# Building the decay of the first seven chunks from operands already on the chip

## The chip, the cores and the metric

One core of a Trainium2 chip runs the whole program. Its engines are TensorE (PE in the profile), VectorE (DVE), ScalarE (ACT), GpSimd (POOL) and SyncE (SP), which only issues transfers here. The metric is the device time of one execution in microseconds (us). Before the change it is 658.33 us, the median of 3 runs (658.04 to 658.83).

## The reference

Three layers follow one another: a chunked state-space scan with 4 batches, 8 heads, 768 positions, head size 32 and state size 16, then a feed-forward layer (256 to 2048 to 256, leaky), then a gated one (256 to 1536 to 256). Only the scan is touched by the change.

```python
log_a = np.log(np.clip(a, 1e-06, 1.0))
for c in range(nc):
    cum = np.cumsum(la, axis=-1)
    L = np.exp(cum[:, :, :, None] - cum[:, :, None, :]) * causal
    CB = np.einsum('bhin,bhjn->bhij', Cc, Bc)
    y_intra = np.einsum('bhij,bhjd->bhid', CB * L, xc)
    y_inter = np.einsum('bhin,bhnd->bhid', Cc, state) * np.exp(cum)[:, :, :, None]
    state = decay_full * state + np.sum(Bx, axis=2)
```

The reference's chunk is 32 positions long; the kernel works with chunks of 96, which gives the same sums.

## The kernel before

The scan has 32 chunks of T = 96 positions (8 per batch). For each chunk four steps are issued. `ev_scores` makes the scores C times B in the PSUM tile `cb`. `ev_decay` makes the exponents cum_i - cum_j plus a causal mask in the PSUM tile `d`, for 8 heads by 96 positions (two products of 384 columns), and ScalarE takes their exponential into `lt`. `ev_weigh` multiplies both into `mt` on VectorE and scales B into `bd`. `ev_out` multiplies `bd` and `mt` with x (tile `yd`); ScalarE copies the new state into the next chunk's x tile `xs` in four small copies and the output into `x1`. `cb` and `d` have one buffer each, so the scores of a chunk wait for the `mt` of the chunk before, and its decay for the `lt` of the chunk before.

The decay product has one left operand `dl` (114 x 112: a unit matrix, two rows of ones, and 16 rows of cum_j, two parts per head) and one right operand `dr` (114 x 768: the mask, two rows of cum_i, and 16 rows of head signs). There are NC = 4 pairs of them. The fixed part of each is copied from `misc` by ScalarE and VectorE (lines 562 to 574); the cum rows come by transfers: for chunks 0 to 2 straight from the tile `parts` (lines 260 to 266), for all later ones through a buffer in device memory, `cum_d` (written at line 291, read at 267 and 270).

The program order is written out by hand: each engine executes its own instructions strictly in the order in which the loop issues them, and SyncE's transfers likewise. The loop runs over chunks i and issues `ev_weigh(i)`, loads of chunk i + 3, `ev_decay(i + 1)`, a share of the weight preparation (`feed`: raw 64-bit words to two 32-bit parts, on VectorE and ScalarE, with raw tiles loaded through GpSimd's queue), `ev_out(i - 1)` and `ev_scores(i + 1)`. After the first 7 chunks, the lead, 512 positions are complete, and from then on each turn also issues a step of the first feed-forward layer (`h` and `acc`). The halves of its first activations are the tiles `xh`; the first half is split by ScalarE and VectorE at chunk 3, the second at chunk 6.

The steps that the change and the prediction touch: the first loads (lines 549 to 560), the set-up of the logarithms, scans and operands (lines 561 to 628), `load_cum` (257), `ev_decay` (297) and the loop's first turns (634 on).

Of the kernel before, what the change touches and what calls it, by code (L numbers as in the profile page):

```python
# [8 lines left out]
F32 = mybir.dt.float32  # L9
# [31 lines left out]
NC = 4  # L41
# [6 lines left out]
def kernel(  # L48
# [159 lines left out]
    DIRECT = 3  # L208
# [13 lines left out]
    picks = x1[0:1, 0, NT - S - 2 * NR:NT - S].rearrange("p (r l) -> p r l", l=2)  # L222
    xs = [apool.tile([W, H * (D + N)], F32, name=f"xs{i}") for i in range(NX)]
# [33 lines left out]
    def load_cum(c):  # L257
        b, k = divmod(c, CPB)
        s = slice(k * T, (k + 1) * T)
        if c < DIRECT:  # L260

            rows = bf(parts[2 * b * H:2 * (b + 1) * H, s])
            for l, e in enumerate((nc.sync, nc.scalar if c < 2 else nc.sync)):
                e.dma_start(out=bf(dr[c % NC][T + l:T + l + 1]), in_=rows[l:2 * H:2])
            nc.sync.dma_start(out=bf(dl[c % NC][T + 2:KD, 0:T]), in_=rows)
            return
# [30 lines left out]
    def ev_decay(c):  # L297

        d = psum.tile([W, 2, 512], F32, tag="d", name="d")
        for e in range(2):  # L300
            nc.tensor.matmul(  # L301
                d[:, e, 0:4 * T], dl[c % NC], dr[c % NC][:, 4 * e:4 * e + 4, :],
                start=True, stop=True,
            )
# [203 lines left out]
    with tc.manual_schedule():  # L508
# [24 lines left out]
        for j in range(NG):  # L533
            nc.gpsimd.memset(ct[j], 0.0)
        warm = apool.tile([2 * NR, 2], F32, name="warm")

        def load_a(e, s):
            for l in range(2):
                e.dma_start(
                    out=a_t[l:2 * NR:2, s], in_=a.rearrange("b h s -> (b h) s")[:, s]  # L540
                )
# [11 lines left out]
        nc.sync.dma_start(out=misc, in_=k_misc[:, c0:])  # L553
        load_bc(0)
        load_x(0)
        take_up(1)
# [4 lines left out]
        seen = apool.tile([128, 2], F32, name="seen")  # L561

        def setup_dl(i):
            nc.scalar.copy(dl[i], left_c)

        def setup_mask(i, e):
            (e.copy if e is nc.scalar else e.tensor_copy)(
                dr[i][0:T], mask_c.unsqueeze(1).broadcast_to([T, H, T])
            )

        def setup_heads(i):
            nc.vector.tensor_copy(
                dr[i][T:KD], heads_c.unsqueeze(2).broadcast_to([KD - T, H, T])
            )
# [8 lines left out]

        clip_a(pieces[0])
        log_a(pieces[0])
        scan(pieces[0])
        setup_heads(0)
        halve_cum(pieces[0], nc.scalar)
        setup_dl(0)
        load_cum(0)  # L590
        clip_a(slice(T, S))
        log_a(slice(T, S))
        setup_mask(0, nc.vector)
        ev_scores(0)
        nc.scalar.activation(warm[:, 1:2], ones_t[:, 0:1], AF.Exp)
        scan(pieces[1])
        halve_cum(pieces[1], nc.vector)
        setup_dl(1)
        setup_mask(1, nc.scalar)
        setup_heads(1)  # L600
        load_bc(1)
        load_cum(1)
        load_x(1)

        nc.gpsimd.tensor_copy(seen[T:KD, 0:1], bf(dl[1][T:KD, 0:1]))
        ev_decay(0)
        take_up(2)
        setup_dl(2)
        setup_mask(2, nc.scalar)
        setup_heads(2)  # L610
        scan(pieces[2])
        load_cum(2)
        halve_cum(pieces[2], nc.vector)
        load_bc(2)
        load_x(2)
        store_cum()
# [7 lines left out]
        for j in range(3, NX):  # L624
            load_eye(j)
# [149 lines left out]
```

## Time and profile before

| | |
|---|---|
| median of 3 runs | 658.33 us |
| the profiled execution's own time | 659.65 us |
| its span, first to last instruction | 657.9 us |
| TensorE busy | 631.5 us (96%) |
| VectorE, ScalarE, GpSimd busy | 389.2, 333.5, 33.5 us |
| mean granted TensorE clock | 0.996 |
| bytes moved | 31.03 MB |

TensorE is busy 96% of the span. The page's slices are 16.4 us long; the first three of them hold most of its idle time. A timeline row gives the start, the length, the engine, the line, what is written from what, the shapes and how many instructions were merged; in brackets stands how long the engine was idle before and what released it.

### The profile page before, as it was taken

Reading aid. Unit: us, or ns where it says so; the run is one execution under the profiler, and the core shown is the slowest. Engines: PE = TensorE matmul, PEld = TensorE weight load, DVE = VectorE, ACT = ScalarE, POOL = GpSimd, SP = SyncE. Lnnn points to the kernel's source line nnn. Section 1 sums busy time; section 2 is a strip of 40 time slices with the busy share of each in tenths; the row PEclk is TensorE's granted clock in tenths of the full one; section 3 lists DMA queues with packets and bytes.
Section 4 is the critical chain, followed back from the end, with each engine's and each line's share of the span. In section 5 each row is a group of like instructions: output and inputs, shape, how many; then the busy total and the mean of one; then the engine's idle time right before and its main releaser. Section 6 shows DMA issues by size and latency. Waiting matters only on the chain.

```text
span 657.9 us, 9595 instructions
## 1 busy us (share of the span) xinstructions
PE 631.5 (96%) x3744; PEld 500.2 (76%) x3744; DVE 389.2 (59%) x636; ACT 333.5 (51%) x628; POOL 33.5 (5%) x54
## 2 busy tenths in 40 slices
PE   2789999999999999999999999999999999999997
PEld 1346666667888888888888888888888888888885
DVE  6489988775887888777586333433433433433432
ACT  5588877776656656665565332332332332332322
POOL 4201101000000000000000000000000000000000
PEclk9989999999999999999999999999999999999999
DMA  4764444410111211220000000100000100100000
GB/s 131 219 203 123 133 127 120 116 55 2 52 45 64 65 50 47 65 64 1 0 1 0 1 1 0 33 1 0 33 0 1 33 0 1 33 0 1 32 1 32
DMA packets 19799, 31.03 MB, mean 47 GB/s; under 512 B 7466, under 2 KB 15274, under 8 KB 19754
## 3 DMA queue, kind: packets, MB, share of 16 engines
q0 software_dynamic: 5152, 17.89, 8.9%
q1 hardware_dynamic: 14394, 12.36, 6.5%
q8 instruction: 29, 0.48, 0.3%
q10 hardware_dynamic: 208, 0.18, 0.1%
q14 instruction: 16, 0.13, 0.1%
HBM read 27.04 MB, written 3.34 MB: 46 GB/s over the span
## 4 chain that ended last, share of the span: by engine, by line
PE 89%; DVE 5%; ACT 3%; issue 1%; DMA 1%; ACTq 0%
PE acc L433 20%; PE h L394 19%; PE gate L460 15%; PE val L460 15%; PE po L488 10%; PE po L493 5%; PE cb L320 3%; PE d L301 1%; DVE mt L327 1%; PE yd L355 1%; DMA dr<-cum_d 1%; PE yd L349 1%; ACT xs L362 1%; DVE raw L168 0%; DVE x L278 0%
## 5 line engine op out<-in xcount | busy, mean ns | idle before, releaser
L394 PE MATMUL h<-xh,win 128*128 128x512 f32 x576 | 146.9, 391 | 1.0 <-ACT xh L385 1.0
L467 DVE TENSOR_TENSOR p<-val,s 128x512 f32<-128x512 f32 x72 | 49.8, 691 | 138.5 <-PE val L460 136.7
L394 PEld LDWEIGHTS h<-xh,win 128*128 128x128 f32 x576 | 107.7, 188 | 22.9 <-ACT xh L385 1.3
L433 PE MATMUL acc<-gh,wout 128*128 128x512 f32 x384 | 105.8, 397 | 0.0
L401 DVE SCALAR_TENSOR_TENSOR g<-h,salpha,t 128x512 f32<-128x512 f32 x96 | 71.9, 749 | 39.6 <-ACT t L399 39.1
L460 PE MATMUL gate<-xh,w2gate 128*128 128x512 f32 x360 | 92.8, 393 | 0.0
L410 ACT CAST gh<-p 128x512 fp32r<-128x512 f32 x72 | 44.6, 620 | 93.5 <-DVE p L467 93.5
L460 PE MATMUL val<-xh,w2val 128*128 128x512 f32 x360 | 91.3, 389 | 0.0
L465 ACT ACTIVATE s<-gate 128x512 f32<-128x512 f32 x72 | 43.0, 597 | 93.1 <-PE gate L460 93.1
L433 PEld LDWEIGHTS acc<-gh,wout 128*128 128x128 f32 x384 | 70.1, 188 | 26.3 <-ACT t L399 11.2
L399 ACT ACTIVATE t<-h,sign 128x512 f32<-128x512 f32 x96 | 66.0, 688 | 42.6 <-PE h L394 41.8
L410 ACT CAST gh<-g 128x512 fp32r<-128x512 f32 x96 | 59.6, 621 | 42.2 <-DVE g L401 42.2
L460 PEld LDWEIGHTS val<-xh,w2val 128*128 128x128 f32 x360 | 67.6, 188 | 14.3
L411 DVE TENSOR_TENSOR gl<-g,gh 128x512 fp32r<-128x512 f32 x96 | 66.0, 688 | 15.3 <-ACT gh L410 14.3
L411 DVE TENSOR_TENSOR gl<-p,gh 128x512 fp32r<-128x512 f32 x72 | 49.7, 691 | 41.2 <-ACT gh L410 41.1
L460 PEld LDWEIGHTS gate<-xh,w2gate 128*128 128x128 f32 x360 | 63.9, 189 | 10.6
L488 PE MATMUL po<-w2out,gh 128*128 128x512 f32 x240 | 64.1, 389 | 0.0
L433 PE MATMUL acc<-gl,wout 128*128 128x512 f32 x192 | 59.2, 390 | 0.0
L488 PEld LDWEIGHTS po<-w2out,gh 128*128 128x128 f32 x240 | 45.0, 188 | 9.4
L433 PEld LDWEIGHTS acc<-gl,wout 128*128 128x128 f32 x192 | 36.0, 188 | 7.9
L493 PEld LDWEIGHTS po<-w2out,gl 128*128 128x128 f32 x240 | 36.7, 189 | 4.7
L493 PE MATMUL po<-w2out,gl 128*128 128x256 f32 x240 | 38.1, 282 | 0.0
(84 smaller groups left out, 566.2 us busy)
## 6 DMA issues: line engine op xcount, KB each, us to landing
raw<-in_moe_w_out_dram POOLq DMA_DIRECT2D x14, 512.0 KB, 4.1
xs<-in_xb_dram SPq DMA_DIRECT2D x32, 144.0 KB
raw<-in_moe_w_in_dram POOLq DMA_DIRECT2D x8, 512.0 KB, 4.8
raw<-in_moe_w_gate_dram POOLq DMA_DIRECT2D x6, 512.0 KB, 4.4
raw<-in_moe_w_val_dram POOLq DMA_DIRECT2D x6, 512.0 KB, 4.1
out_dram<-osb SPq DMA_DIRECT2D x12, 256.0 KB
bt<-in_bc_dram SPq DMA_DIRECT2D x7, 192.0 KB
ct<-in_bc_dram SPq DMA_DIRECT2D x28, 48.0 KB
```

What stands on the lines that cost most here:

```text
L320: nc.tensor.matmul(cb[:, e, 0:4 * T], left, right, start=True, stop=True)
L394: nc.tensor.matmul(h, w[:, wl, kt, :], xh["m1", k][:, xl, kt, :], start=(i == 0 and kt == 0), stop=(i == 2 and kt == KT - 1),)
L399: nc.scalar.activation(t, h, AF.Identity, scale=sign[:, f:f + 1])
L401: nc.vector.scalar_tensor_tensor(g, h, salpha[:, f:f + 1], t, op0=ALU.mult, op1=ALU.max)
L410: nc.scalar.copy(gh, g)
L411: nc.vector.tensor_tensor(gl, g, bf(gh), op=ALU.subtract)
L433: nc.tensor.matmul(acc[k][:, m], w[:, wl, m * 128:(m + 1) * 128], g, start=(first and i == 0), stop=(last and i == 2),)
L460: nc.tensor.matmul(p, w[:, wl, kt, :], xh["m2", k][:, xl, kt, :], start=(i == 0 and kt == 0), stop=(i == 2 and kt == KT - 1),)
L465: nc.scalar.activation(s, gate, AF.Sigmoid)
L467: nc.vector.tensor_tensor(p, val, s, op=ALU.mult)
L488: nc.tensor.matmul(o[e][:, u].rearrange("p (l d) -> p l d", l=2), ph[:, ts], w, start=(f == 0), stop=False, skip_group_check=True,)
L493: nc.tensor.matmul(o[e][:, u, 0:DM], pl[:, ts], w[:, 0, :], start=False, stop=last, skip_group_check=True,)
```

## The change

For chunks 0 to 6 (`DIRECT = 7`) the decay is no longer built from `dl` and `dr`. A left operand `early_l` holds, for all seven chunks side by side, the unit matrix and the 16 rows of cum_j, which VectorE copies from `parts`; a right operand `early_r` holds the mask and the head signs. One product of 384 columns gives the mask and the cum_j part; the cum_i part is added by four products of 96 columns with `early_i` (16 x 112 per head) on the left and `parts` on the right. With two halves a chunk has two products of 384 and eight of 96 columns. The three operands lie in weight tiles (`win[-1]`, `wout[-1]`, `wout[-2]`) that are not yet in use. The direct transfers from `parts` into `dl` and `dr` are gone; chunks 7 and later still use `dl` and `dr`, of which there are now 3 pairs, set up by `setup_decay` in the loop at chunks 1 to 3. The scans of positions 288 to 767 move behind `ev_weigh(0)`. The logarithms come in two pieces at the start, the loads of a, misc, B, C and x are issued in another order, and GpSimd clears `ct[1]` after its first weight load.

```diff
+            if c >= DIRECT:
+                nc.tensor.matmul(
+                    d[:, e, 0:4 * T], dl[c % NC], dr[c % NC][:, hs, :], start=True, stop=True
+                )
+                continue
             nc.tensor.matmul(
-                d[:, e, 0:4 * T], dl[c % NC], dr[c % NC][:, 4 * e:4 * e + 4, :],
-                start=True, stop=True,
-            )
+                d[:, e, 0:4 * T], early_l[:, c], early_r[:, hs, :],
+                start=True, stop=False, skip_group_check=True,
+            )
+            for q in range(4):
+                nc.tensor.matmul(
+                    d[:, e, q * T:(q + 1) * T], early_i[:, 4 * e + q],
+                    parts[0:2 * H, c * T:(c + 1) * T],
+                    start=False, stop=True, skip_group_check=True,
+                )
...
-        load_a(nc.sync, pieces[0])
-        load_a(nc.scalar, slice(T, S))
-        nc.scalar.dma_start(out=pick, in_=picks)
+        for l, e in enumerate((nc.sync, nc.scalar)):
+            e.dma_start(out=a_t[l:2 * NR:2], in_=a.rearrange("b h s -> (b h) s"))
+        nc.sync.dma_start(out=pick, in_=picks)
+        nc.scalar.dma_start(out=misc, in_=k_misc[:, c0:])
+        nc.scalar.dma_start(out=neg, in_=k_misc[T + 2:KD, c0:c0 + H])
...
+        nc.gpsimd.memset(ct[1], 0.0)
+        take_up(2)
...
         clip_a(pieces[0])
         log_a(pieces[0])
+        clip_a(rest)
+        log_a(rest)
+        nc.scalar.activation(
+            early_i, neg.unsqueeze(2).broadcast_to([2 * H, H, W]), AF.Copy, scale=-1.0
+        )
+        nc.scalar.copy(
+            early_l[0:T], left_c[0:T].unsqueeze(1).broadcast_to([T, DIRECT, W])
+        )
...
+        def later_cum():
+            scan(pieces[2])
+            halve_cum(pieces[2], nc.scalar)
+            early_cum(pieces[2])
+            store_cum()
+            for j in range(3, NX):
+                load_eye(j)
+            setup_alpha()
+
+        def setup_decay(j):
+
+            nc.scalar.copy(dl[j], left_c)
+            nc.scalar.copy(dr[j][0:T], mask_c.unsqueeze(1).broadcast_to([T, H, T]))
+            nc.sync.dma_start(out=bf(dr[j][T + 2:KD]), in_=bf(early_r[T:W]))
...
             if i == 0:
+                later_cum()
+            if i == 1:
...
-            if i + 4 < NCH:
-                load_cum(i + 4)
+            if DIRECT <= i + 3 < NCH:
+                load_cum(i + 3)
...
+            if 0 < i <= NC:
+                setup_decay(i - 1)
```

TensorE, from the values of chunk 0 (`yd`) to the scores of chunk 3 (`cb`), before; `d` is the decay of chunk 3 there:

```order
L349 MATMUL yd<-xs_102,bd 16x32 x8
L355 MATMUL yd<-mt,xs_102 32x96 x8
L320 MATMUL cb<-bct 112x384 x2
L301 MATMUL d<-dr_115,dl_111 112x384 x2
L349 MATMUL yd<-xs_103,bd 16x32 x8
L355 MATMUL yd<-mt,xs_103 32x96 x8
L320 MATMUL cb<-bct 112x384 x2
```

The same place after; `wout_89` is the tile under `early_r`, `win_81` that under `early_l`, `wout_88` that under `early_i`:

```order
L362 MATMUL yd<-xs_103,bd 16x32 x8
L368 MATMUL yd<-mt,xs_103 32x96 x8
L333 MATMUL cb<-bct 112x384 x2
L308 MATMUL d<-wout_89,win_81 112x384
L313 MATMUL d<-parts,wout_88 112x96 x4
L308 MATMUL d<-wout_89,win_81 112x384
L313 MATMUL d<-parts,wout_88 112x96 x4
L362 MATMUL yd<-xs_104,bd 16x32 x8
L368 MATMUL yd<-mt,xs_104 32x96 x8
L333 MATMUL cb<-bct 112x384 x2
```

The decay between the scores of chunk 2 and the values of chunk 1 has grown from two products to ten, of which eight have 96 columns.

ScalarE, from the exponential of chunk 2 to the output copy of chunk 1, before (`mag` and `win` are weight preparation):

```order
L306 ACTIVATE lt<-d 112x768
L362 COPY xs_103<-yd 16x2x32 x4
L363 COPY x_73<-yd 128x2x96
L133 ACTIVATE mag<-raw 128x512
L306 ACTIVATE lt<-d 112x768
L148 CAST win_74<-mag 128x512
L362 COPY xs_104<-yd 16x2x32 x4
L363 COPY x_73<-yd 128x2x96
```

And after:

```order
L319 ACTIVATE lt<-d 112x768
L375 COPY xs_104<-yd 16x2x32 x4
L376 COPY x_73<-yd 128x2x96
L133 ACTIVATE mag<-raw 128x512
L631 CAST dl_109<-misc 114x112
L632 CAST dr_112<-misc 96x768
L319 ACTIVATE lt<-d 112x768
L148 CAST win_74<-mag 128x512
L375 COPY xs_105<-yd 16x2x32 x4
L376 COPY x_73<-yd 128x2x96
```

The two copies that fill a `dl` and a `dr` now stand between the weight scaling and the exponential of chunk 3; before, all of them stood ahead of the loop. The same pair stands once more in each of the next two turns.

SyncE, from the store of the cum rows on, before:

```order
L291 DMA cum_d<-parts 64x768
L267 DMA dl_111<-cum_d 16x96
L270 DMA dr_115<-cum_d 2x8x96
L237 DMA xs_105<-in_xb_dram 96x384
L246 DMA bct<-in_bc_dram 128x496
L267 DMA dl_108<-cum_d 16x96
L270 DMA dr_112<-cum_d 2x8x96
```

And after:

```order
L292 DMA cum_d<-parts 64x768
L245 DMA xs_106<-in_xb_dram 96x384
L254 DMA bct<-in_bc_dram 128x496
L245 DMA xs_107<-in_xb_dram 96x384
L257 DMA bt_115<-in_bc_dram 128x4x96
L263 DMA ct_117<-in_bc_dram 32x384 x4
L633 DMA dr_112<-wout_89 16x768
```

Behind the store, the cum rows of chunks 3 and 4 stood between the loads of x and C; now the loads of x, B and C follow at once.

## Rows read from the trace of the kernel before

**Rows 1.** Page, slices: busy tenths of TensorE in 40 slices of 16.4 us
```profile
PE   2789999999999999999999999999999999999997
```

**Rows 2.** Windows: length, busy us of PE, PEld, DVE, ACT, POOL, clock, DMA share, GB/s
```profile
20.00:30.00 10.00, 5.92 (x56) 2.42 (x59) 3.67 (x8) 4.10 (x13) 2.10 (x4) 1.00 0.89 257
...
30.00:40.00 10.00, 8.47 (x140) 4.17 (x136) 8.01 (x17) 8.21 (x23) 1.72 (x3) 0.83 0.60 173
...
50.00:60.00 10.00, 10.00 (x103) 6.67 (x102) 9.96 (x19) 8.36 (x20) 1.42 (x2) 1.00 0.44 126
```

**Rows 3.** Chain of waits, first 60 us: start, length, what
```profile
19.71 4.46 DMA dr<-cum_d
```

**Rows 4.** Timeline, TensorE: start, length, line, tile, shapes, idle before and releaser
```profile
6.24 1.62 PE L320 MATMUL cb<-bct 64*112 64x384 f32 x4 [6.24 <-DMA bct<-in_bc_dram]
...
10.38 0.95 PE L301 MATMUL d<-dr,dl 114*112 114x384 f32 x2 [2.51 <-DMA dl<-parts]
...
24.30 0.95 PE L301 MATMUL d<-dr,dl 114*112 114x384 f32 x2 [2.93 <-DMA dr<-cum_d]
...
32.15 0.60 PE L301 MATMUL d<-dr,dl 114*112 114x384 f32 x2
...
36.05 0.98 PE L301 MATMUL d<-dr,dl 114*112 114x384 f32 x2
...
42.77 1.67 PE L394 MATMUL h<-xh,win 128*128 128x512 f32 x6 [1.00 <-ACT xh L385]
...
44.95 0.90 PE L320 MATMUL cb<-ct,bt 64*112 64x384 f32 x4
```

**Rows 5.** Timeline, VectorE: the products mt of chunks 0 to 4
```profile
14.51 0.95 DVE L327 TENSOR_TENSOR mt<-cb,lt 112x768 f32<-112x768 f32 x1
...
17.18 0.96 DVE L327 TENSOR_TENSOR mt<-cb,lt 112x768 f32<-112x768 f32 x1 [0.86 <-PE cb L320]
...
21.48 0.96 DVE L327 TENSOR_TENSOR mt<-cb,lt 112x768 f32<-112x768 f32 x1 [1.81 <-PE cb L320]
...
29.04 0.96 DVE L327 TENSOR_TENSOR mt<-cb,lt 112x768 f32<-112x768 f32 x1 [1.67 <-PE cb L320]
...
33.85 0.95 DVE L327 TENSOR_TENSOR mt<-cb,lt 112x768 f32<-112x768 f32 x1
```

**Rows 6.** Timeline, VectorE, from 10.7 to 16 us: scans, cum halves, alpha, weights
```profile
10.73 1.34 DVE L278 TENSOR_TENSOR_SCAN x<-ones_t,x 64x96 f32<-64x96 f32 x5
...
12.55 0.71 DVE L286 SCALAR_TENSOR_TENSOR parts<-x,pick 64x480 fp32r<-64x480 f32 x1
...
13.88 0.22 DVE L370 TENSOR_SCALAR sign<-alpha_sb 128x16 f32<-128x16 f32 x1
...
15.57 0.42 DVE L158 TENSOR_SCALAR raw<-raw 128x512 uint32<-128x512 uint32 x1
```

**Rows 7.** Timeline, ScalarE: exponential, set-up copies, state copies, split of the first activations
```profile
11.37 0.81 ACT L306 ACTIVATE lt<-d 112x768 f32<-112x768 f32 x1 [0.65 <-PE d L301]
...
12.98 0.28 ACT L564 CAST dl<-misc 114x112 fp32r<-114x112 f32 x1
...
13.17 0.83 ACT L567 CAST dr<-misc 96x768 fp32r<-96x768 f32 x1
...
19.88 0.84 ACT L362 COPY xs<-yd 16x64 f32<-16x64 f32 x4 [0.15 <-PE yd L355]
...
31.82 0.32 ACT L363 COPY x<-yd 128x192 f32<-128x192 f32 x1
...
32.60 0.61 ACT L385 CAST xh<-x 128x512 fp32r<-128x512 f32 x1
```

**Rows 8.** Timeline, TensorE: weight load of decay products, value products of a chunk
```profile
10.35 0.45 PEld L301 LDWEIGHTS d<-dr,dl 114*112 114x112 f32 x2 [3.66 <-ACT dl L564]
...
18.96 0.85 PE L355 MATMUL yd<-mt,xs 112*32 112x96 f32 x16
```

**Rows 9.** Page, costliest groups: the narrow products of the last stage
```profile
L493 PE MATMUL po<-w2out,gl 128*128 128x256 f32 x240 | 38.1, 282 | 0.0
```

More of the change, by code (lines that the diff above doesn't have):

```diff
@@ L40 @@
 NX = 6
-NC = 4
+NC = 3
 NG = 2
@@ L259, in load_cum @@
         s = slice(k * T, (k + 1) * T)
[L260 to L266, printed above, removed]
         nc.sync.dma_start(
@@ L532 @@
         nc.vector.memset(ones_t, 1.0)
-        for j in range(NG):
-            nc.gpsimd.memset(ct[j], 0.0)
+        nc.gpsimd.memset(ct[0], 0.0)
         warm = apool.tile([2 * NR, 2], F32, name="warm")
[L537 to L540, printed above, removed]
-                )
         def load_eye(i):
@@ L560 @@
         nc.gpsimd.dma_start(out=units_c, in_=k_misc[:, 0:N])
[L561 to L574, printed above, removed]
+        nc.gpsimd.memset(ct[1], 0.0)
+        take_up(2)
+        load_bc(2)
+        load_x(2)
+        load_eye(2)
+        take_up()
         def clip_a(s):
@@ L582, in log_a, with early_cum @@
             nc.scalar.activation(a_t[:, s], cum[:, s], AF.Ln)
+        def early_cum(s):
+            cs = slice(s.start // T, min(s.stop // T, DIRECT))
+            nc.vector.tensor_copy(
+                early_l[T:W, cs, 0:T],
+                bf(parts[0:2 * H, cs.start * T:cs.stop * T]).rearrange("p (c t) -> p c t", t=T),
+            )
+        rest = slice(T, S)
         clip_a(pieces[0])
         log_a(pieces[0])
-        scan(pieces[0])
-        setup_heads(0)
-        halve_cum(pieces[0], nc.scalar)
@@ L589 @@
[L589 to L593, printed above, removed]
+        clip_a(rest)
[6 more added lines that the diff above has]
+        )
+        nc.scalar.activation(warm[:, 1:2], ones_t[:, 0:1], AF.Exp)
+        nc.vector.tensor_copy(
+            early_l[T:W, :, T:W],
+            ct[0][T:W, 0, 0:DIRECT * N].rearrange("p (c n) -> p c n", n=N),
+        )
@@ L594 @@
+        nc.vector.tensor_copy(early_r[T:W], neg.unsqueeze(2).broadcast_to([2 * H, H, T]))
+        scan(pieces[0])
+        halve_cum(pieces[0], nc.vector)
+        early_cum(pieces[0])
+        nc.vector.tensor_copy(early_r[0:T], mask_c.unsqueeze(1).broadcast_to([T, H, T]))
         ev_scores(0)
[L595 removed]
+        ev_decay(0)
         scan(pieces[1])
         halve_cum(pieces[1], nc.vector)
[L598 to L599 removed]
@@ L600 @@
[L600 to L616, printed above, removed]
-        load_eye(2)
-        nc.gpsimd.tensor_copy(seen[T:KD, 1:2], bf(dl[2][T:KD, 0:1]))
@@ L619 @@
-        take_up()
-        setup_dl(3)
-        setup_mask(3, nc.scalar)
-        setup_heads(3)
-        load_cum(3)
-        for j in range(3, NX):
-            load_eye(j)
-        setup_alpha()
+        early_cum(pieces[1])
+        def later_cum():
[10 more added lines that the diff above has]
+            nc.sync.dma_start(out=bf(dr[j][T + 2:KD]), in_=bf(early_r[T:W]))
```

11 lines of the change are left out of this document (9 added, 2 removed).

## The prediction

> **What bounds the kernel now.** I read the page's slices first: TensorE is full from the fourth of 40 slices to the end, so only the first 50 us hold time that a change of the scan's start could give back [rows 1]. The windows show the same more finely: TensorE works 5.92 of the 10 us from 20 to 30, 8.47 from 30 to 40, and all of 50 to 60, while VectorE has 9.96 in that last stretch [rows 2]. The order of the work behind the lead is the same before and after. What counts is therefore when the first product of the feed-forward layer starts, 42.77 us in the profiled execution [rows 4]: whatever the lead gains or loses, the end gains or loses.
>
> The chain of waits names one large piece in the lead that the change removes: 4.46 us from the issue of the cum_i row of chunk 3 until it has landed, and TensorE stands idle 2.93 us for it before the decay at 24.30 [rows 3, 4]. The starts of the products `mt` give the pace of the chunks: 14.51, 17.18, 21.48, 29.04, 33.85 us [rows 5]. The step from chunk 2 to chunk 3 takes 7.6 us where its neighbours take 4.3 and 4.8.
>
> The clock has to be read with them. The granted clock stands at 1.00 in the window from 20 to 30 [rows 2], yet the same decay takes 0.95 us at 10.38 and 24.30 and 0.60 us at 32.15, and four score products take 1.62 us at 6.24 and 0.90 us at 44.95 [rows 4]. I take the long durations for the lower level (1.2 GHz) and the short ones for 2.4 GHz. From 30 to 40 us the granted clock reads 0.83 on average, and at 36.05 the decay takes 0.98 again [rows 2, 4]. TensorE thus runs most of the lead at the lower level, and what the change adds there is added at the dear price.
>
> **What one small product costs.** Each of the first seven chunks gets eight products of 96 columns with a weight load of 112 columns each. No row shows this form. The nearest ones bound it. From below: 16 value products of 96 columns, with loads of only 32, take 0.85 us [rows 8], 0.053 each, and each value product appears as two of them: 0.106 us at the lower level, half of that, about 0.066 with some floor, at the higher. From above: half a decay of 384 columns, 0.95 / 2 = 0.48 and 0.60 / 2 = 0.30 us [rows 4]. In between stand the load itself, 0.45 / 2 = 0.225 us at the lower level for 112 columns [rows 8], and the narrowest single product with a load of this kind, 38.1 / 240 = 0.159 us at the higher level [rows 9]. I take 0.16 at the higher level, the row nearest in kind, and 0.28 at the lower, between the load's 0.225 and twice 0.159. A decay then takes 0.95 + 8 x 0.28 = 3.2 us at the lower level and 0.60 + 8 x 0.16 = 1.9 at the higher, where it took 0.95 and 0.60. It can't get cheaper than it was, since both wide products stay.
>
> The Trainium skill, page "TensorE: Matmul & The Clock Gate", section "LDWEIGHTS (loading the stationary operand)", says that a weight load's time goes by its columns and not by its rows, 1 / 1.2 ns a column. By that the sixteen rows of a small product are loaded no faster than the 114 of a decay, and 112 columns would be 93 ns, an estimate from that page. The trace's load takes 225 ns at the lower level, so here the measurement decides; with 93 ns a product the sum below would be a gain of about 6 us instead of 1.9.
>
> **The start, to the first `mt`.** Removed: the scatter of the cum rows of chunk 0 by three transfers, for the last of which the decay at 10.38 waited [rows 4]. Added ahead of it on ScalarE: the second logarithm and two fills; by 0.83 us for 768 columns and 0.28 for 112 [rows 7] a fill of 896 costs 0.94 and one of 784 0.84. Both a transfers are now whole (98 KB); I expect them no more than some tenths later than the small piece was, and this is covered, since the operands are ready at about 7.3 us while TensorE is in the first scores until 7.86 [rows 4]. The decay of chunk 0 then runs from 7.86 to 11.05, the exponential (0.81 [rows 7]) to 11.9, and the first `mt` starts at 11.9 instead of 14.51: 2.6 us won.
>
> **Chunks 1 and 2 give it back.** VectorE now does between `mt(0)` and `mt(1)` what it did before the loop: five scans 1.34, the cum parts 0.71, a cast on ScalarE between them 0.6, a copy of cum_j 0.3 (a 384-column fill), alpha 0.6 (13.88 to 14.51), two weight operations 0.42 each, the weighing itself 0.95 [rows 5, 6], and the scaling of B, priced like the 112-column copy at 0.28 [rows 7]: 5.65 us, less some 0.08 where neighbours overlap, 5.3. So `mt(1)` starts at 17.2 instead of 17.18. TensorE has decay 1 (11.9 to 15.1), scores 1 (1.62, to 16.7), decay 2 (to 19.9) without a gap. I assume that such unbroken work brings the higher level at about 17 us, so that from then on values take about 0.75, scores 0.9, a decay 1.9: values 0 to 20.7, scores 2 to 21.6, and `mt(2)` at 21.6 against 21.48. Up to here nothing is won.
>
> **Chunks 3 to 6.** No transfer stands in front of decay 3: 21.6 to 23.45, against 24.30 before. `mt(3)` follows at 25.4 against 29.04, decay 4 at 25.1, its exponential ends at 27.8. Here the second cost comes: the set-up of `dl` and `dr`, 0.28 + 0.83 = 1.11 us of ScalarE [rows 7], was done where ScalarE waited and now stands in each of the turns 1, 2 and 3; in turn 3 it stands right ahead of the first split `xh`. State copies 0.84, output copy 0.32, a weight scaling (priced like the split), set-up 1.11 and the split 0.61 [rows 7], overlaps of 0.1 taken off, are 3.1 us and end at 30.9, and `mt(4)` starts at 31.6 against 33.85. Chunks 5 and 6 keep this distance (decay 6 takes 1.9, but at the higher level, where it took 0.98 before), and the first feed-forward product starts at 40.5. Followed row by row in the same way, the kernel before comes to 42.4 where the trace has 42.77, so the difference that I trust is 42.4 - 40.5 = 1.9 us. Without the three set-ups it would be 2.9.
>
> **Edits at no cost, and their cover.** Weight tiles 1 to 3 are loaded some 6 us earlier beside B, C and x; the DMA engines are 0.89 busy from 20 to 30 before [rows 2], and this spreads that load forward. If the loads crowd each other instead, scores 1 or `bd(0)` wait. Three pairs of `dl` and `dr` instead of four: each load is issued one turn later and has two turns, 9 us, before its decay, against 4.46 for the slowest landing [rows 3]. SyncE loses the scatter transfers and three loads through device memory and gains three fills of `dr`, which have two turns. GpSimd clears `ct[1]` behind the first weight load and nobody needs it before chunk 8.
>
> **Sum.** The profiled execution took 659.65 us with a span of 657.9; the span goes to 656.0, the execution to 657.75. The profiled execution lies 1.32 over the median 658.33, so for the median I forecast 656.4.
>
> **Rivals.** (1) TensorE becomes the bound, the slower side: the higher level comes late, as before, where the 5.92 us of work in the stretch 20 to 30 did not bring it [rows 2, 4]. Decays 1 to 4 at 3.2 us each then run behind one another with scores and values. With the rise at 25 us the same chain gives 0.5 us lost, at 28.5 us 1.5, at 32 us 3.2; with products at the upper bounds 3.75 even with an early rise. It decides from a rise at about 24 us or a small product over 0.35. For it: small products of sixteen rows may count as little work. Against: there is no gap between 11.9 and 20. I set 660.5. (2) The small products cost near the lower bound: `mt(2)` comes at 19 and the whole distance stays; 5.8 us won, 652.6. For it: they may overlap with their neighbours' loads. Against: the load row of 0.225. (3) It doesn't do what it says for the time: the wait for the transfer goes, but its 1.8 us at decay 3 are spent on set-ups and small products, or crowded first loads delay chunks 1 and 2; nothing over 1 us remains, 657.8.
>
> **How the numbers follow.** Forecast 0.50, rival 1 0.17, rival 2 0.14, rival 3 0.19. Of this kernel a difference under about 0.2% (1.3 us) can't be told from none. The forecast's own range is 654.4 to 657.6 (rise at 15 to 22 us: 3.9 to 0.8 won); 0.42 of its half lies over 1.3 us won, 0.08 under. Faster: 0.42 + 0.14 = 0.56. Same: 0.08 + 0.18 = 0.26, nearly all of rival 3 among it. Slower: rival 1 and the rest, 0.18. The range takes in half of rival 2 and most of rival 1: 653.3 to 660.0.
>
> **What would show it.** Right: the first `mt` near 12 us, the second still near 17, no wait of TensorE for a transfer in front of decay 3, `mt(3)` near 25.5, the first product `h` near 41, short durations of TensorE from 17 to 20 us on. The price of a small product is read directly, as decay length less 0.95 or 0.60, divided by eight. Wrong: decays of 3 us and more after 25 us, or `h` later than 42.8; or, the other way, decays near 1.5 us at the lower level and `h` before 38. If the shift at `h` does not reappear at the end, the idea that the rest only moves along is wrong.

## The result and the profile after

The changed kernel takes 666.82 us (median of 4 runs, 666.02 to 666.88), the kernel before on the same chip 658.58 us (658.04 to 659.71): 1.0119 times as long, with a 95% interval of 1.0103 to 1.0135. The forecast was 656.4 us, so it is wrong, on the slower side and outside its range. The profiled execution took 666.88 us with a span of 665.1. Some executions of a kernel take several per cent longer or more; the ratios below leave them out, and of b3 and k1, whose profiles fell on such executions (714.40 and 799.34 us), only the first 22 us are read.

The page's busy tenths of TensorE show an engine that is full earlier than before [rows 1]:

```profile
PE   4999999999999999999999999999999999999996
```

The windows of the changed kernel (columns as in [rows 2]: length, busy us of PE, PEld, DVE, ACT, POOL, clock, DMA share, GB/s) say from when:

```profile
10.00:20.00 10.00, 9.10 (x30) 5.84 (x29) 6.73 (x21) 3.60 (x7) 2.32 (x4) 1.00 0.57 185
20.00:30.00 10.00, 10.00 (x90) 5.96 (x90) 4.90 (x10) 6.70 (x18) 0.73 (x1) 1.00 0.65 188
30.00:40.00 10.00, 10.00 (x91) 5.97 (x90) 5.01 (x11) 6.25 (x18) 1.02 (x2) 1.00 0.42 119
40.00:50.00 10.00, 10.00 (x90) 5.56 (x89) 6.31 (x13) 6.01 (x17) 0.92 (x2) 1.00 0.31 92
```

Where TensorE had 5.92 and 8.47 us of work in the stretches 20 to 30 and 30 to 40 [rows 2], it now has 10.00 in each up to 50 us, with VectorE half idle. TensorE has become the bound of the lead. The transfer share fell from 0.89 to 0.65 in the first of them.

The timeline of TensorE (start, length, line, tile, shapes, and in brackets the idle time before) answers to [rows 4]. L333 are the scores, L308 a wide half of a decay, L313 its four small products, L304 a decay from `dl` and `dr`, L407 the first feed-forward product:

```profile
9.44 0.63 PE L308 MATMUL d<-wout,win 112*112 112x384 f32 x1 [2.22 <-DVE wout L613]
10.00 0.98 PE L313 MATMUL d<-parts,wout 16*112 16x96 f32 x4
...
42.18 0.98 PE L313 MATMUL d<-parts,wout 16*112 16x96 f32 x4
...
45.63 0.98 PE L304 MATMUL d<-dr,dl 114*112 114x384 f32 x2
...
47.52 1.63 PE L333 MATMUL cb<-ct,bt 64*112 64x384 f32 x4
49.08 0.60 PE L304 MATMUL d<-dr,dl 114*112 114x384 f32 x2
49.60 1.63 PE L407 MATMUL h<-xh,win 128*128 128x512 f32 x6
```

The reader is to see two things. All durations up to 48 us are the long ones (scores 1.63, a plain decay 0.98), that is the 1.2 GHz level; the first short decay, 0.60, stands at 49.08, where the kernel before had one at 32.15. The clock column of the windows reads 1.00 throughout, so it can't be trusted here: the durations decide (e3 below has the same durations under a clock of 0.50). And `h` starts at 49.60 instead of 42.77, 6.83 us later. From there to the last instruction it is 665.1 - 49.60 = 615.5 us, before it was 657.9 - 42.77 = 615.1: the loss is made in the lead and passes to the end whole.

In the chain of waits (start, length, what) of the changed kernel the 4.46 us for the cum_i row [rows 3] are gone. Instead every turn of the lead is TensorE alone:

```profile
29.08 0.59 PE d L308
29.67 0.91 PE d L313 x4
30.58 0.59 PE d L308
31.17 0.91 PE d L313 x4
32.08 0.34 PE yd L362 x16
32.42 0.64 PE yd L368 x16
33.06 1.56 PE cb L333 x4
34.62 0.59 PE d L308
```

A turn is 34.62 - 29.08 = 5.54 us: decay 3.00, values 0.98, scores 1.56. Four small products take 0.91, one 0.228 us. The products `mt` of chunks 0 to 3 on VectorE start 5.51, 4.79 and 5.47 us apart (answer to [rows 5]):

```profile
13.36 0.96 DVE L340 TENSOR_TENSOR mt<-cb,lt 112x768 f32<-112x768 f32 x1 [2.35 <-ACT lt L319]
...
18.87 0.96 DVE L340 TENSOR_TENSOR mt<-cb,lt 112x768 f32<-112x768 f32 x1
...
23.66 0.96 DVE L340 TENSOR_TENSOR mt<-cb,lt 112x768 f32<-112x768 f32 x1 [2.30 <-PE cb L333]
...
29.13 0.96 DVE L340 TENSOR_TENSOR mt<-cb,lt 112x768 f32<-112x768 f32 x1 [0.46 <-PE cb L333]
```

Up to `mt(3)` the changed kernel is level with the one before (29.13 against 29.04); all of the loss shows after it (`mt(4)` starts at 36.92, before at 33.85).

### The profile page after: what moved, and what is told of

Read it like the earlier page. It is cut to its first block, busy times and chain, and to the rows that moved or that the text cites. A ratio compares the mean times of both kernels' runs of the same rounds, so it can differ in the third digit from the quotient of the medians.

```text
span 665.1 us, 9677 instructions
## 1 busy us (share of the span) xinstructions
PE 649.0 (98%) x3800; PEld 513.6 (77%) x3800; DVE 390.1 (59%) x637; ACT 335.5 (50%) x629; POOL 32.8 (5%) x52
## 4 chain that ended last, share of the span: by engine, by line
PE 93%; DVE 4%; ACT 2%; DMA 1%; ACTq 0%; issue 0%
PE acc L446 20%; PE h L407 18%; PE gate L473 15%; PE val L473 15%; PE po L501 10%; PE po L506 5%; PE cb L333 4%; PE d L313 2%; PE yd L368 1%; PE d L308 1%; PE d L304 1%; PE yd L362 1%; DVE mt L340 1%; DMA neg<-in_k_misc_dram 1%; DVE raw L168 0%; DVE g L414 0%
## 5 line engine op out<-in xcount | busy, mean ns | idle before, releaser
L407 PE MATMUL h<-xh,win 128*128 128x512 f32 x576 | 146.9, 391 | 0.0
L407 PEld LDWEIGHTS h<-xh,win 128*128 128x128 f32 x576 | 107.7, 188 | 21.7 <-DVE g L414 0.4
L319 ACT ACTIVATE lt<-d 112x768 f32<-112x768 f32 x32 | 26.0, 812 | 26.3 <-PE d L304 11.9
```

What stands on the lines that cost most here:

```text
L407: nc.tensor.matmul(h, w[:, wl, kt, :], xh["m1", k][:, xl, kt, :], start=(i == 0 and kt == 0), stop=(i == 2 and kt == KT - 1),)
```

## The experiments

Theory: the small products make TensorE the bound, because its clock stays at the lower level while they run. Rivals: the set-ups of `dl` and `dr`, the later start, the price of a small product by itself. The table has all runs, each ratio against the kernel before on the same chip. "h" is the start of the first feed-forward product and "short" the first decay of a length that the 2.4 GHz level gives, both in the profiled execution.

| run | us | ratio (95% interval) | h | short |
|---|---|---|---|---|
| changed kernel | 666.82 | 1.0119 (1.0103 to 1.0135) | 49.60 | 49.08 |
| e1_no_small | 654.29 | 0.9925 (0.9908 to 0.9941) | 38.22 | 22.50 |
| e6_start | 665.91 | 1.0109 (1.0093 to 1.0125) | 48.53 | 47.91 |
| e7_setup_first | 666.29 | 1.0115 (1.0099 to 1.0132) | 48.52 | 47.27 |
| e2_rows64 | 666.35 | 1.0106 (1.0091 to 1.0121) | 48.51 | about 48 |
| e4_blocks | 664.15 | 1.0072 (1.0057 to 1.0087) | 46.40 | 45.15 |
| e3_fill | 662.84 | 1.0061 (1.0038 to 1.0084) | 45.59 | 8.26, again 44.23 |
| e5_turnfill | 660.39 | 1.0024 (1.0001 to 1.0048) | 40.42 | 8.93 |
| b2_turnfill | 660.32 | 1.0022 (1.0010 to 1.0034) | 41.51 | 9.71 |
| e9_wide112 | 655.97 | 0.9957 (0.9942 to 0.9971) | 38.89 | 20.87 |
| e10_narrow112 | 661.38 | 1.0033 (1.0022 to 1.0044) | 43.73 | 42.86 |
| e11_wide8 | 659.18 | 0.9998 (0.9989 to 1.0006) | 41.76 | 17.47 |
| e8_direct4 | 659.27 | 1.0003 (0.9993 to 1.0014) | 41.17 | 30.78 |
| b3_direct4 | 657.84 | 0.9977 (0.9966 to 0.9988) | not read | not read |
| k1_block128 | 658.56 | 0.9993 (0.9984 to 1.0002) | not read | not read |
| k2_hybrid | 659.20 | 1.0007 (0.9996 to 1.0018) | 41.32 | 19.79 |
| k3_hybrid5 | 661.18 | 1.0039 (1.0024 to 1.0053) | 43.28 | 32.89 |
| k4_loads_first | 656.33 | 0.9963 (0.9950 to 0.9976) | 39.14 | 29.08 |

In every profile that was read, the span less `h` is 615.1 to 615.8 us. So `h` alone tells what a profiled execution gained or lost; some 1.1 us of it is the start, which differs between executions even where no edit touched it (see e6 and e7).

**The small products away (e1_no_small).**

```diff
-            for q in range(4):
-                nc.tensor.matmul(d[:, e, q * T:(q + 1) * T], early_i[:, 4 * e + q], ...)
```

> The eight products of 96 columns are left out, so the decay of the first seven chunks lacks cum_i; all else is as in the changed kernel. Theory (the small products hold TensorE at the lower level and make it the bound of the lead): without them the turn of 5.54 us falls to that of the other engines, the clock rises before 35 us, the first product h starts between 36 and 39.5 us instead of 49.6, and the time falls to 653 to 657 us. Rival (the later first mt, 13.4 us, and the three set-ups on ScalarE cost the time): h stays beyond 46 us, the time above 663 us.

654.29 us and `h` at 38.22, as the theory had it. The small products cost 666.82 - 654.29 = 12.5 us, and all that the change does beside them gains 659.18 - 654.29 = 4.9 us against the kernel before on that chip (0.75%). The timeline of TensorE shows the level rise early:

```profile
19.40 0.98 PE L308 MATMUL d<-wout,win 112*112 112x384 f32 x2
...
22.50 0.60 PE L308 MATMUL d<-wout,win 112*112 112x384 f32 x2
...
38.22 1.66 PE L401 MATMUL h<-xh,win 128*128 128x512 f32 x6 [0.68 <-ACT xh L392]
```

At the lower level a decay takes 0.91 us from start to start here (19.40 to 20.31) and 3.00 in the changed kernel, 2.09 more, in seven chunks 14.6. `h` moves by 11.38 only, for without the small products TensorE is not the bound everywhere: the scores at 29.47 wait 2.96 us for `mt`. How much is added work and how much the level, e1 doesn't say; e5 tells them apart.

**Start and set-ups (e6_start, e7_setup_first).** VectorE's copy of the head signs behind the mask, and the two ScalarE fills exchanged; or the three set-ups ahead of the loop.

```diff
         # e6
+        nc.vector.tensor_copy(early_r[T:W], neg...)   # now behind the mask's copy
         # e7
-            if 0 < i <= NC:
-                setup_decay(i - 1)
+        for j in range(NC):            # ahead of ev_scores(0)
+            setup_decay(j)
```

> The changed kernel with two orders swapped: the copy of the head signs on VectorE, which waited for its late transfer and held the scans behind it, moves behind the mask copy, and on ScalarE the fill of the unit matrix goes ahead of the one that waits for the same transfer. Theory (TensorE is the bound from the second decay on): the first mt starts 1 to 2 us earlier than 13.4 us and the whole shift reaches the end, time 664.8 to 665.8 us, h at 47.6 to 48.6. Rival (the start is covered by VectorE's chain behind the first mt): the time stays at 666.5 us.

> The changed kernel with the three set-ups of dl and dr on ScalarE moved ahead of the first decay, where ScalarE waits from 8.9 to 12.5 us. Theory (TensorE is the bound of the lead, ScalarE waits for it): no difference, 666.0 to 667.4 us, h within 0.5 us of 49.6. Rival (the set-ups stand in the path, as the prediction had it at 1.0 us): 664.5 to 665.8 us.

In the profiles `h` came 1.07 and 1.08 us earlier, with the first decay at 8.37 and 8.54 us (9.44 in the changed kernel) and `mt(0)` at 12.29 and 12.47 instead of 13.36. Neither time is told apart from the changed kernel's 666.82: the intervals overlap. For e7 all but 0.2 us of the shift is the start, which its edit doesn't touch: from `mt(0)` to `h` it takes 36.05 us, the changed kernel 36.24. So the set-ups are worth 0.2 us at most, although its `h` missed the 0.5 us that were expected.

The start itself differs from execution to execution. In the changed kernel GpSimd's clearing of `ct[1]` and VectorE's copy of the head signs overlap:

```profile
5.60 1.38 POOL L570 MEMSET ct<- 128x1536 f32 x1
...
5.74 1.65 DVE L609 CAST wout<-neg 16x768 fp32r<-16x768 f32 x1 [1.08 <-DMA neg<-in_k_misc_dram]
```

In e7 the copy comes before the clearing, which begins at 5.77:

```profile
5.05 0.55 DVE L609 CAST wout<-neg 16x768 fp32r<-16x768 f32 x1
```

Where `neg` had landed before the clearing began (e7, and likewise e2, e8, e10), the copy took 0.55 us and the first decay started at 8.30 to 8.54; where both began within 0.2 us of each other (the changed kernel, e1, e9, e11, k4), the copy took 1.62 to 1.84 us and the first decay started at 9.35 to 9.59. e6 has the copy behind the clearing, at 7.67, and 0.55 us too. So e6's own effect can't be read from one profile, and that the clearing slows the copy is read from the overlap; no run moved the clearing.

**Rows and width (e2_rows64, e4_blocks).** The small products over 64 rows, 48 of them zero; or one product of 16 rows and 384 columns in place of four, its right operand a block pattern that VectorE writes in 0.94 us per chunk.

```diff
         # e2
-                nc.tensor.matmul(d[...], early_i[:, 4 * e + q], parts[0:2 * H, ...])   # early_i: 16 rows
+                nc.tensor.matmul(d[...], early_i[:, 4 * e + q], parts[0:64, ...])      # early_i: 64 rows
         # e4, in place of the four
+            nc.tensor.matmul(d[:, e, 0:4 * T], ones_i, blk[c % 2][:, hs, :], ...)
```

> The small products run over 64 rows instead of 16 (48 rows of zeros on the left); nothing else changes but one fill with zeros. If the clock stays low because a product of 16 rows counts as little work, the short durations appear by 25 to 30 us and h starts at 40 to 45 us, time 657 to 662 us. If it stays low because of the idle time between short products whatever their rows, or if the bound is elsewhere, h stays within 1 us of 49.6 and the time within 0.3% of 666.8 us.

> The eight small products of a chunk become two of 384 columns and 16 rows, whose right operand VectorE builds (cum_i of each head in its own block, others zero; one operation of 16 x 768 a chunk). Theory: a decay takes 1.95 us at the lower level instead of 3.0, TensorE is no longer the bound or only just, h starts at 38 to 44 us, time 655 to 661 us. Rival (start and set-ups): h beyond 46 us. VectorE's seven operations of about 0.8 us are an extra cost that may take 1 to 3 us of it.

Rows of zeros change nothing: a turn is still 5.54 us, and `h` comes 1.09 us earlier by the early start (first decay at 8.30). The blocks shorten a turn from 5.54 to 4.90 us (a decay 4 x 0.59), and that is all: TensorE is still full and still at the lower level until 44 us. Its theory missed, with 664.15 us for 655 to 661 and `h` at 46.40 for 38 to 44: it had expected that TensorE would no longer, or only just, be the bound.

**Dense products in the gaps (e3_fill, e5_turnfill, b2_turnfill).** bf16 products of 128 rows and 512 columns on zeros: 10 at the start, 6 and 4 around the first decay (e3); also 4 in each of the turns 0 to 5 (e5); the like in the kernel before (b2).

```diff
+        fill(10)                       # at the start
         ev_scores(0)
+        fill(6)
         ev_decay(0)
+        fill(4)
+            if i <= 5:                 # e5 and b2 only: in each turn, behind the scores
+                fill(4)
```

> Twenty dense products of 512 columns on zeros are added to the changed kernel on TensorE alone: ten at the start, six after the first scores, four after the first decay, where TensorE waits. Theory (the level is what makes the small products dear): the level is high by 6 to 9 us; if it then lasts, a decay takes about 1.7 us, h starts near 38.5 to 40 us and the time is 655 to 657 us; if the small products cannot keep it, it falls back within the first chunks and h is 45 to 50 us. Rival (start and set-ups): h stays beyond 46 us with decays short.

> The changed kernel with the twenty dense products on zeros of the run before and four more in each of the first six turns, behind the scores, where TensorE waits for an exponential. Theory (at the lower level, which the small products don't lift, TensorE is the bound): the level stays high, a decay takes 1.75 us, a turn 1.75 + 0.75 + 0.9 + 0.9 = 4.3 us instead of 5.54, h starts at 40 to 43 us and the time is 656 to 659 us although there is more work. Rival (small products cost by their number whatever the level): h at 49 us or later, time 667 us or more.

> The kernel before with the same dense products on zeros (ten at the start, eight behind the first scores, four behind the first decay, four in each of the first six turns). Theory: the level alone moves the lead: products shorten by some 2 us between 10 and 32 us, but the wait for the cum_i row of chunk 3 at 24.3 us and for the B and C of chunk 3 at 27.3 us stay, so h moves from 42.77 to 40 to 42 us, time 655.5 to 658 us. Rival (the level has no part in it): 658 to 660 us.

With the fills at the start alone (e3, its second case), TensorE holds the higher level until 15.7 us, and the timeline shows the price of a small product at both levels, four of them at a time:

```profile
8.59 0.59 PE L314 MATMUL d<-parts,wout 16*112 16x96 f32 x4
9.11 0.43 PE L309 MATMUL d<-wout,win 112*112 112x384 f32 x1
...
15.66 0.66 PE L309 MATMUL d<-wout,win 112*112 112x384 f32 x1
16.25 0.98 PE L314 MATMUL d<-parts,wout 16*112 16x96 f32 x4
```

From start to next start four take 9.11 - 8.59 = 0.52 us, 0.13 each. Behind the fills the level falls, at 15.7 us, and it stays down until 42.8 us under an unbroken stream. Here the clock column shows it, 0.50 in the windows from 20 to 40 us, over the same durations (0.66 for a wide product, 0.98 for four small ones) that the changed kernel has under 1.00:

```profile
20.00:30.00 10.00, 10.00 (x91) 6.38 (x91) 5.38 (x11) 5.70 (x17) 1.25 (x3) 0.50 0.46 132
```

With fills in each turn (e5) all durations are short from the first scores on, and `h` stands at 40.42, 9.2 us earlier, although TensorE has more to do: the level, not the number of products, is what the changed kernel loses most by. That profiled execution took 657.73; the median, 660.39, is above the 659 that were expected. The nine runs behind the ratio scatter from 657.41 to 663.67, the longer ones with a lower mean granted clock (0.986 to 0.994 against 0.998 and 0.999), so the fills are no cure. In the kernel before (b2) they gain nothing either, and 660.32 us lies above both its cases: decay 3 still waits 2.23 us for its transfer, and at 18.13 a decay takes 1.20 us, so the level had fallen again.

**What in the products does it (e9_wide112, e10_narrow112, e11_wide8).** All three leave the small products out and add products with a left operand of zeros over 112 rows: one of 384 columns per half, four of 96 per half, three of 384 per half.

```diff
+            for q in range(3):         # e11; once in e9; four of 96 columns in e10
+                nc.tensor.matmul(d[:, e, 0:4 * T], early_z, early_r[:, hs, :], start=False, ...)
```

> The changed kernel with each four small products (16 rows, 96 columns) replaced by one more wide product of the kind that is there already (112 rows, 384 columns) with zeros for its left operand, so the decay lacks cum_i. TensorE issues the same four wide products per decay as in the kernel with blocks of 16 rows (turns of 4.9 us at the lower level, short durations from 44.2 us, h at 46.40). If products of few rows keep the level down: the first short durations by 25 us, turns of 4.0 us or less, h at 39 to 41, 655 to 658 us. If it is not the rows but a mix in which the decay's and the scores' products stand alone: the lower level until 40 us and later, h at 45 to 46.5, 662 to 664.

> The changed kernel with its eight small products kept in number and width (96 columns, weight load of 112) but over 112 rows with a left operand of zeros, so the decay lacks cum_i. If narrow products with a load each are what costs: four in 0.91 us, turns of 5.5 us, no short decay before 44 us, h at 47 to 49, 664 to 667. If it is the 16 rows (their change against the 112 rows of the wide product beside them): four in 0.6 us or less, turns of 4.2 or less, short durations by 25 us, h at 39 to 42, 655 to 659.

> The kernel with wide products of zeros over 112 rows, three of them instead of one per half, so a decay has eight wide products and takes TensorE at least as long at the lower level (0.46 + 7 x 0.32 = 2.7 us, by the rows of the kernel with four) as with the small ones (3.0). If the added time alone kept the level down: turns of 5.2 us, no short duration before 44 us, h at 45 to 48, 662 to 666. If work of this kind raises it: short durations by 22 us though TensorE is the bound at first, h at 39 to 41.5, 656 to 659.

The two rows of e11 (TensorE, three wide products of zeros) lie a chunk apart:

```profile
13.74 1.16 PE L313 MATMUL d<-wout,wout 112*112 112x384 f32 x3
...
17.74 0.69 PE L313 MATMUL d<-wout,wout 112*112 112x384 f32 x3
```

Its decay of eight wide products takes 16.11 - 13.28 = 2.83 us at the lower level, nearly the 3.00 of the changed kernel, and still the level rises at about 17 us (`h` at 41.76 and 659.18 us are 0.3 and 0.2 beyond that case's ranges). So it is not the added time. In e10 the four narrow products take 0.65 us instead of 0.91 (20.76 to 21.41), a turn 4.84 instead of 5.54, and yet the lower level stays:

```profile
20.76 0.84 PE L313 MATMUL d<-wout,wout 112*112 112x96 f32 x4
...
42.86 0.60 PE L304 MATMUL d<-dr,dl 114*112 114x384 f32 x2
```

TensorE is busy 10.00 and 9.97 us in its stretches 20 to 30 and 30 to 40. The expectation for e10 met neither of its cases in full: the 16 rows cost 0.07 us of the 0.228, but with the narrow form alone the level stayed down too. e9 had promised the durations of e4 and did not have them: its decay takes 1.55 us (12.08 to 13.63), where e4's takes 2.36, so by itself it told less than e11 does. With wide products of 112 rows the level rose at 20.9 (e9) and 17.5 us (e11); with narrow ones of 112 rows (e10) and wide ones of 16 rows (e4) it stayed down until 42 and 44. What the chip looks at in them is not settled by these runs.

**Fewer chunks with small products (e8_direct4).** The edit of e7 and one number.

```diff
-    DIRECT = 7
+    DIRECT = 4
```

> Small products in chunks 0 to 3 only, chunks 4 to 6 from dl and dr as before the change (with the three set-ups ahead of the loop). Theory (TensorE is the bound at the lower level, each chunk pays for itself): four small products take 0.91 us, so a chunk 1.82, and three chunks fewer give 5.5 us: h at 43.1, 660.8 us. If the higher level comes back as soon as the small products stop, at about 30 us, 2 us more: 658.8. Rival (the loss was made in the first chunks, and the later ones are only moved along): no more than 1 us, 665 or more.

659.27 us, some 7 us under e7. The last small products start at 24.59, the scores at 29.94 are short (0.91). That is near the theory's better case, in which the level comes back at about 30 us (658.8). How the 7 us split between three chunks without small products and the earlier rise is not separated.

**Versions with the whole computation.** In the kernel before, chunk 3's rows straight from `parts` (b3_direct4). In the changed one, chunks 1 to 6 over 128 rows with blocks by VectorE (k1_block128); or small products for chunks 0 and 1 only, chunks 2 and 3 scattered from `parts` (k2_hybrid), chunk 4 too (k3_hybrid5), and the loads of chunks 3 and 4 ahead of those scatters (k4_loads_first). k2 to k4 also have the set-ups ahead of the loop, as in e7. The diff shows only the lines that matter most.

```diff
-    DIRECT = 3
+    DIRECT = 4                         # b3, in the kernel before
+            if c > 0:                  # k1
+                nc.tensor.matmul(d[:, e, 0:4 * T], all_l[:, c - 1], all_r[c % 2][:, hs, :], ...)
-    DIRECT = 7
+    DIRECT = 2                         # k2 to k4
+        load_cum(2)                    # k2 to k4: three transfers from parts
+        for j in (3, 4):               # k4
+            load_x(j)
+            load_bc(j)
...
+            load_cum(3)                # in later_cum; load_cum(4) too in k3 and k4
             store_cum()
```

> The kernel before with one number changed: chunk 3 too gets its cum rows straight from the parts on the chip by three transfers, not through device memory. Theory (TensorE's idle 2.93 us in front of decay 3 was a real loss that a cheaper edit can take): the store's leg of the transfer goes, about 2 us, decay 3 at 22.3 instead of 24.3, and 656.5 us. Rival (the lead is set by the work of VectorE and ScalarE or by the clock, not by this wait): 658 to 659, no change. Rival (three transfers with short pieces land no sooner): no change either, with the wait still in the chain.

> Chunk 0 as in the changed kernel; for chunks 1 to 6 cum_i comes as sixteen more rows of the one wide product: the right operand gets sixteen rows of head by head blocks, written by VectorE (0.94 us per chunk in the kernel with blocks), the left one gets its cum_j rows by two transfers. TensorE then has two wide products per decay, as in the kernel without the small ones. Theory (the small products kept TensorE at the lower level and made it the bound): h at 38 to 40 us, about 655.5 us (654.3 of the kernel without them, and some of VectorE's 0.94 us ahead of the second mt). Rival (the VectorE work of six blocks, 5.6 us, moves onto the path): h at 42.5 to 44, 658.5 to 660. Rival (rows of blocks hold the level down as well, as in the kernel with blocks): no short decay before 40 us, 661 or more.

> Small products in chunks 0 and 1 only; chunks 2 and 3 get their cum rows by three transfers each straight from the parts on the chip, the later ones from device memory; the set-ups stand ahead of the loop. Theory (each chunk with small products costs TensorE 1.82 us at the lower level, and the early start and the missing wait in front of decay 3 are worth some 5 us): two chunks with them lie in the time in which VectorE holds up mt(1) at 17.7 anyway, mt(2) at 20.6 instead of 22.7, mt(3) at 24 to 25, h at 39 to 40, about 655.5 us. Rival (a transfer becomes the wait again, as in the kernel with chunk 3 scattered, or the set-ups and VectorE hold the later turns): h at 41 to 42, 657.5 to 658.5. Rival (gains of the lead are lost behind h): h before 40 and still 658.

> As the kernel with small products in chunks 0 and 1 only, but chunk 4 too gets its cum rows by three transfers straight from the parts, issued right behind those of chunk 3. In that kernel TensorE stood idle for 5.12 us in front of decay 4, whose rows from device memory were issued at 23.26 and landed 4.75 us later. Theory (that wait is what the early start had turned into): decay 4 at about 23.5 instead of 28.25, decay 5 at about 28 with the next load as the likeliest new wait, h at 37.5 to 39.5 instead of 41.32, 655 to 656.5 us. Rival (the next load, of chunk 5, lands as late as that of chunk 4 did): decay 5 not before 28 to 30, h at 40 to 41, 657.5 to 658.5. Rival (the lead no longer sets the end): h before 40 and no less than 658.5.

> As the kernel with chunks 2 to 4 scattered from the parts, but the loads of x, B and C of chunks 3 and 4 are issued ahead of the scatters of chunks 3 and 4, behind which they waited on SyncE's queue (issue of B and C of chunk 3 at 21.69, landed 6.77 us later, TensorE idle 6.20 for it). Theory (this queue is what the gain of the early start is lost to): scores 3 at about 22 instead of 28.59, decay 4 at 24 to 26, h at 38 to 40, 655 to 656.5 us. Rival (the wait moves on once more, to the rows of chunk 5 from device memory): h at 40.5 to 42, 657 to 658.5. Rival (the early loads delay the rows of chunk 2 or the weights): mt(2) later than 22, 659 or more.

b3 is 0.23% faster than the kernel before, by one number; 657.84 us lies between its theory and its rivals. In the first 22 us of its profile decay 3 starts at 21.01 with no wait in front. k1, 658.56 us, comes to the time of its first rival: decay 1 waits 3.76 us for its transfer, and `mt(1)` comes at 19.12 (16.84 in e1). k2 and k3, at 659.20 and 661.18 us with `h` at 41.32 and 43.28, met none of their cases in full: the wait moved on. The rows of TensorE with the idle time in brackets, k2 first:

```profile
28.25 0.95 PE L311 MATMUL d<-dr,dl 114*112 114x384 f32 x2 [5.12 <-DMA dl<-cum_d]
```

```profile
28.59 1.63 PE L340 MATMUL cb<-bct 64*112 64x384 f32 x4 [6.20 <-DMA bct<-in_bc_dram]
```

Both come from the order in which SyncE issues the transfers. In k2 the rows of chunk 4 are issued only at 23.26, behind the loads of x, B and C; in k3 those loads are issued from 21.02 on, behind the scatters, which wait for `parts`. With the loads first (k4) the same places read:

```profile
24.30 1.63 PE L340 MATMUL cb<-bct 64*112 64x384 f32 x4
26.08 0.95 PE L311 MATMUL d<-dr,dl 114*112 114x384 f32 x2 [0.16 <-ACT x L383]
...
39.14 1.65 PE L414 MATMUL h<-xh,win 128*128 128x512 f32 x6 [0.92 <-ACT xh L405]
```

656.33 us and `h` at 39.14, as its theory had it: 0.9963 (0.9950 to 0.9976) of the kernel before, the lowest ratio with the whole computation, and by the two ratios (0.9963 / 1.0119) about 1.5% under the changed kernel. Its interval overlaps that of b3 (0.9966 to 0.9988), which changes one number.

## Why the prediction was wrong

**The step that failed** is "I assume that such unbroken work brings the higher level at about 17 us". The work was unbroken, from 13.38 to the feed-forward layer, and the level came at 49. From the values of chunk 0 on, the sum then ran with values of 0.75, scores of 0.9 and decays of 1.9 us where the trace has 0.98, 1.56 and 3.00. Both signs that the prediction had named for being wrong came, decays of 3 us after 25 us and `h` later than 42.8. e5 shows that this step carries the miss: where all durations were short, `h` came at 40.42 (forecast 40.5) and the span was 656.0 (forecast 656.0). That they agree to the tenth is partly luck: e5 has the higher level from its first scores on and 44 products more, and its `mt(3)` and `mt(4)` start at 23.61 and 30.23, where the sum had 25.4 and 31.6.

The Trainium skill, page "TensorE: Matmul & The Clock Gate", section "What's actually happening", says that the clock follows how busy TensorE has been of late. The trace does not bear that out as it stands: TensorE is 10.00 of 10 us busy, as the profile counts it, in each window from 20 to 50 us, and the level is the lower one until 49; in e10 it is busy 10.00 and 9.97 us from 20 to 40, and the level is the lower one until 42. The measurement decides.

**Rival 1** named the mechanism rightly (TensorE the bound at the lower level) and sized it too small. It took the rise of the kernel before, about 32 us, as the latest one, a loss of 3.2 us, and the range ended at 660.0, below the rival's own 660.5. But in the runs the rise came at 17 to 49 us with different products, and the products were what the change altered. With the rise at 49 the loss is 8.2 us at the median. Its reason, the sixteen rows, is not the whole of it: with 64 and 112 rows (e2, e10) the level stayed down until 48 and 42 us.

**The price of a small product** was taken at 0.28 and 0.16 us. Read as the prediction said, decay length less the old one, divided by eight, it is (3.00 - 0.95) / 8 = 0.256 at the lower level and, from e5's first decay of 1.73 us, (1.73 - 0.60) / 8 = 0.14 at the higher: both within their bounds and cheaper, so this term is not what made the forecast too low. The small product itself takes 0.228 and 0.13; the rest is the wide product beside it. The weight load's row, 0.225 [rows 8], was the right neighbour.

**The start.** The decay of chunk 0 began at 9.44 instead of 7.86 us and `mt(0)` at 13.36 instead of 11.9. The chain of waits names what I left out, the transfer of `neg`:

```profile
2.25 3.47 DMA neg<-in_k_misc_dram
```

Behind it VectorE copies the head signs (5.74 to 7.39, above), and only then come the scan and the mask:

```profile
7.42 0.35 DVE L279 TENSOR_TENSOR_SCAN x<-ones_t,x 64x96 f32<-64x96 f32 x1
...
8.62 0.67 DVE L613 CAST wout<-misc 96x768 fp32r<-96x768 f32 x1
```

The clearing of `ct[1]`, which stood among the edits at no cost, began 0.14 us before that copy; without the overlap the first decay starts at 8.30 to 8.54 (e2, e7, e8), still later than forecast.

Between `mt(0)` and `mt(1)` I summed 5.3 us and the trace has 5.51; that step held.

**The wait removed** is gone as forecast, no transfer stands in front of decay 3, and the early part of the change is worth its gain (e1). **The set-ups**, 1.11 us each, priced at 1 us in the path, cost 0.2 us at most (e7). In turn 3 they do hold up the split `xh` and `mt(4)`, 36.92, but the scores that wait for `mt(4)` start at 38.53 right behind TensorE's own work. **The shift at `h`** passes to the end whole, as assumed.

## What to carry to other kernels

Work that is added to an engine on which two clock levels were seen is to be priced at the lower one, unless the trace shows that this very kind of work has run at the higher one; that the engine was busy without a gap was no evidence here. Replace a wait by many narrow products only where the engine has that time to spare at the lower level, and in as few chunks as the wait needs. When one wait in a lead is taken away, read the next one off the queue that issues the loads before you count the gain: here it moved twice before the order of the loads of x, B and C settled it. And try the smallest edit that removes the wait first: b3 changes one number and can't be told from the best version.

## What the runs showed of the hardware

- In the changed kernel TensorE ran at the 1.2 GHz level until 49 us while the windows show it busy 10.00 of 10 us from 20 to 50; its decays had products of 96 columns over 16 rows, with a load each. Over 64 rows (e2) or 112 (e10), or with 384 columns over 16 rows (e4), the lower level lasted until 48, 42 and 44 us. With products of 384 columns over 112 rows in their place the level rose at 20.9 (e9) and 17.5 us (e11).
- At the lower level a wide product (112 rows, 384 columns) takes 0.32 us behind another of the same rows (e9, e11) and 0.59 beside one of 16 rows (the changed kernel, e4); four narrow ones over 112 rows take 0.65 and over 16 or 64 rows 0.91 us.
- A VectorE copy of 16 x 768 took 1.65 us at 5.74 us in the changed kernel, while GpSimd cleared a tile of 128 x 1536, and 0.55 us at 5.05 in e7, before the clearing. In e5 the copy began first, at 5.65, and took 0.55; the clearing, begun at 5.76, took 1.77 us instead of 1.38.
- The clock column can read 1.00 over a stretch in which every duration is of the lower level (the changed kernel to 49 us); in e3, where the higher level came first, it reads 0.50 over the same durations.
